# Values of one group directly behind the scores of the next: a change of the order of work around eight PSUM banks

## The chip, the cores and the metric

The kernel runs on one core of a Trainium2 chip. The metric is the device time of one execution in microseconds, median of several; all runs told here are of the same (fast) state, except `e8_before_again`, a single run whose state is not known. Engines are called as in the profile: PE is TensorE, DVE is VectorE, ACT is ScalarE, POOL is GpSimd.

## The reference

Attention with a sliding window of 128 and four sink tokens, then a gated feed-forward block on its output:

```python
# q, k, v: batch 4, 8 heads, 768 tokens, head size 64; n_sink 4, window 128
scores = q @ k.T / sqrt(64)
keep = (key < 4) | ((0 <= query - key) & (query - key < 128))
a = softmax(where(keep, scores, -1e9)) @ v
x = a.transpose(0, 2, 1, 3).reshape(3072, 512)          # w_gate, w_val: 512x1536
out = (silu(x @ w_gate) * (x @ w_val)) @ w_out           # w_out: 1536x512
```

## The kernel before

Tokens come in 12 groups of 256 (g; three to a batch, c is the place in the batch), a group in two tiles of 128 (j). `step_S` makes the scores of one half of the heads and takes four PSUM banks, `step_K` the scores against the sink tokens, `step_PV` the values of one tile and one half of the heads:

```python
    def step_PV(g, j, hh, act=False):
        b, c = divmod(g, GC)
        ...
        po = bank([P, 4, D + 1], FP32, "o")
        mms = []
        if c > 0:
            mms.append((po, es_t[g][:, j * P:(j + 1) * P],
                        vsbs[b][:, 4 * hh:4 * hh + 4]))
        for hq in range(4):
            h = 4 * hh + hq
            if t > 0:
        ...
        for i, (o, l, r) in enumerate(mms):
            nc.tensor.matmul(o, l, r, start=(i == 0), stop=(i == len(mms) - 1),
                             skip_group_check=True)

        def dve():
            rcp = smallp.tile([P, 4, 1], FP32, tag="rcp", name="rcp")
            nc.vector.reciprocal(rcp, po[:, :, D:D + 1])
            ...                              # or on ScalarE, at the start
            nc.vector.tensor_tensor(
                xns[g, j][:, 256 * hh:256 * (hh + 1)].rearrange(
                    "p (h d) -> p h d", h=4),
                po[:, :, 0:D], rcp.broadcast_to([P, 4, D]), op=ALU.mult)
        later.append(dve)                    # runs at the next flush
```

The feed-forward block works in eight token blocks. A unit of it is a `gate`: projection pg, tanh on ScalarE, then whatever attention steps the plan puts there, then projection pv; VectorE forms u (from tanh and pg) and ht (from u and pv), and then does the attention's masks and normalisations that were put off:

```python
        pg = project(wgs, "pg")
        th = tpool.tile([P, 512], FP32, tag="th", name="th")
        nc.scalar.activation(th, pg, AF.Tanh, scale=0.5)
        for a in attn:
            a()
        pv = project(wvs, "pv")
        ...
            nc.vector.scalar_tensor_tensor(u, th, 1.0, pg, op0=ALU.add, op1=ALU.mult)
            nc.vector.tensor_tensor(hts[tb][...], u, pv, op=ALU.mult)
        ...
            product()
            flush()
```

All PSUM tiles come from one pool of eight banks (`psum = pool("psum", 8, True)`), and which bank a tile gets is settled when the program is built. The plan of the later stages spreads scores (two steps, two units apart) and values (four half tiles in four units):

```python
    def pair(ga, gb, sh=0):
        s = sh
        return [((s, s + 2), Ss(ga)), ((s + 4, s + 5, s + 6, s + 7), PVs(ga)),
                ((s + 6, s + 8), Ss(gb)),
                ((11, 11, 12, 12) if s else (10, 11, 12, 13), PVs(gb))]

    weave(gates(3) + downs(3), slots(
        (2, [K(5)]), *pair(5, 6, 2), (2, C(6)), (7, C(7)), (13, C(8))))
    weave(gates(4) + downs(4), slots(
        (0, sinks(2)), *pair(7, 8), (3, [K(7)]), (3, C(9)), (7, C(10)), (10, C(11))))
    weave(gates(5) + downs(5), slots(
        (0, sinks(3)), *pair(9, 10), (6, [K(10)])))
    weave(gates(6) + gates(7) + downs(6) + downs(7), slots(
        ((0, 2), Ss(11)), ((4, 5, 6, 7), PVs(11))))
```

I call the stretch from the first gate projection of token block 3 to that of block 4 "stage 3", and so on; the part after stage 5 is the "last part".

The softmax here doesn't subtract the row's maximum and nothing guards it: scores larger than these inputs give would overflow.

## Time and profile before

| | value |
|---|---|
| time, median of 3 | 242.3 us (241.95 to 242.7) |
| profiled span | 240.4 us, mean granted clock 0.993 |
| TensorE busy | 97% of the span |
| TensorE idle in stages 3 to 5 (78.66 to 187.43 us) | none: its view of waits in that window is empty |
| VectorE busy | 66% |

How to read such a page: TensorE's row is the one that counts, as it is busy all the time from 25 us on. There a removed matmul or a cheaper form gains its length, and a wait costs its length. The lines themselves are in the prediction.

### The profile page before, as it was taken

Reading aid. Unit: us, or ns where it says so; the run is one execution under the profiler, and the core shown is the slowest. Engines: PE = TensorE matmul, PEld = TensorE weight load, DVE = VectorE, ACT = ScalarE, POOL = GpSimd, SP = SyncE. Lnnn points to the kernel's source line nnn. Section 1 sums busy time; section 2 is a strip of 40 time slices with the busy share of each in tenths; the row PEclk is TensorE's granted clock in tenths of the full one; section 3 lists DMA queues with packets and bytes.
Section 4 is the critical chain, followed back from the end, with each engine's and each line's share of the span. In section 5 each row is a group of like instructions: output and inputs, shape, how many; then the busy total and the mean of one; then the engine's idle time right before and its main releaser. Section 6 shows DMA issues by size and latency. Waiting matters only on the chain.

```text
span 240.4 us, 5190 instructions
## 1 busy us (share of the span) xinstructions
PE 232.7 (97%) x2071; PEld 135.3 (56%) x2071; DVE 158.8 (66%) x334; ACT 112.6 (47%) x227; POOL 70.7 (29%) x92
## 2 busy tenths in 40 slices
PE   7799999999999999999999999999999999999994
PEld 3477887768745445454445454445454445488443
DVE  4569778939973589880698971498971599877000
ACT  2778447358451483621656611556611662332111
POOL 8985387686256745650000000000000000000000
PEclk9979999999999999999999999999999999999999
DMA  7999999999999999999920654200304200200132
GB/s 136 147 180 197 206 187 206 171 154 145 194 119 200 195 160 155 155 148 191 236 48 0 125 97 133 87 0 1 46 0 131 90 0 3 44 0 3 59 117 87
DMA packets 98793, 27.37 MB, mean 114 GB/s; under 512 B 84817, under 2 KB 95825, under 8 KB 98769
## 3 DMA queue, kind: packets, MB, share of 16 engines
q0 software_dynamic: 68832, 13.90, 71.5%
q1 hardware_dynamic: 29504, 12.75, 26.9%
q10 hardware_dynamic: 432, 0.39, 0.5%
q8 instruction: 16, 0.26, 0.5%
q14 instruction: 9, 0.07, 0.1%
HBM read 28.34 MB, written 6.29 MB: 144 GB/s over the span
## 4 chain that ended last, share of the span: by engine, by line
PE 87%; DVE 5%; ACT 3%; DMA 2%; issue 1%; DVEq 0%; ACTq 0%; POOLq 0%
PE pv L448 25%; PE pd L501 25%; PE pg L448 23%; PE o L384 5%; PE s L331 4%; PE pt L267 3%; ACT e L338 2%; DVE e L343 2%; DMA kq<-in_k_dram 2%; DVE ht L463 1%; DVE xn L396 1%; PE px L420 1%; DMA out_dram<-ot 1%; DVE u L462 1%; ACT xn L392 1%
## 5 line engine op out<-in xcount | busy, mean ns | idle before, releaser
L448 PE MATMUL pv<-xT,wv 128*128 128x256 bf16 (+1 forms) x384 | 74.4, 326 | 0.2 <-DVE xn L396 0.2
L448 PE MATMUL pg<-xT,wg 128*128 128x256 bf16 (+1 forms) x384 | 74.2, 326 | 0.0
L455 ACT ACTIVATE th<-pg 128x512 f32<-128x512 f32 x72 | 43.9, 609 | 59.7 <-PE pg L448 59.3
L462 DVE SCALAR_TENSOR_TENSOR u<-th,pg 128x512 bf16<-128x512 f32 x72 | 49.2, 683 | 30.5 <-ACT th L455 29.7
L501 PE MATMUL pd<-wo,ht 128*128 128x512 bf16 x276 | 63.4, 379 | 0.0
L463 DVE TENSOR_TENSOR ht<-u,pv 128x512 bf16<-128x512 bf16 x72 | 49.5, 687 | 10.2 <-PE pv L448 3.3
L448 PEld LDWEIGHTS <-wg 128*128 128x128 bf16 x384 | 37.4, 98 | 25.4 <-issue 0.2
L338 ACT ACTIVATE e<-s 128x512 bf16<-128x512 f32 (+1 forms) x96 | 46.3, 583 | 1.2 <-PE s L331 1.1
L448 PEld LDWEIGHTS <-wv 128*128 128x128 bf16 x384 | 34.1, 98 | 20.6 <-issue 2.7
L501 PEld LDWEIGHTS <-ht 128*128 128x128 bf16 x276 | 25.8, 98 | 28.0 <-issue 0.2
L505 ACT ACTIVATE ot<-pd 128x512 f32<-128x512 f32 x23 | 13.7, 597 | 53.0 <-PE pd L501 52.9
L343 DVE TENSOR_TENSOR e<-e,mask 128x1024 bf16<-128x1024 bf16 (+1 forms) x48 | 28.9, 641 | 1.2 <-ACT e L338 1.0
L123 POOL DMA_DIRECT2D va<-in_v_dram x24 | 21.2, 885 | 12.6 <-DMA kq<-in_q_dram 5.7
L384 PEld LDWEIGHTS <-e 128*128 128x128 bf16 x352 | 16.6, 99 | 6.7 <-DVE vcf L598 0.7
L396 DVE TENSOR_TENSOR xn<-o,rcp 128x256 bf16<-128x256 f32 x44 | 18.7, 424 | 2.5 <-DMA xT<-xn 1.0
L384 PE MATMUL o<-va,e 128*128 128x65 bf16 x352 | 18.2, 195 | 0.9 <-DVE vcf L598 0.5
L107 POOL DMA_DIRECT2D kq<-in_k_dram x16 | 14.1, 883 | 8.6 <-DMA kqT<-kq 4.5
L107 POOL DMA_DIRECT2D kq<-in_q_dram x16 | 14.1, 883 | 6.1 <-DMA va<-in_v_dram 2.9
L389 DVE RECIPROCAL rcp<-o 128x4 f32<-128x4 f32 x48 | 8.4, 176 | 6.8 <-PE o L384 6.8
L486 DVE TENSOR_SCALAR ot<-pd 128x256 f32<-128x256 f32 x1 | 0.4, 425 | 14.4 <-DMA out_dram<-ot 14.4
L331 PE MATMUL s<-kqT 64*128 64x128 bf16 (+1 forms) x168 | 9.4, 238 | 0.0
L272 DVE CAST qT<-pt 128x512 bf16<-128x512 f32 x7 | 4.7, 689 | 6.9 <-PE pt L267 6.9
(61 smaller groups left out, 107.5 us busy)
## 6 DMA issues: line engine op xcount, KB each, us to landing
out_dram<-ot SPq DMA_DIRECT2D x23, 256.0 KB
va<-in_v_dram POOLq DMA_DIRECT2D x24, 128.0 KB, 10.3
kq<-in_k_dram POOLq DMA_DIRECT2D x18, 128.0 KB, 9.3
kq<-in_q_dram POOLq DMA_DIRECT2D x16, 128.0 KB, 9.4
wo<-in_moe_w_out_dram POOLq DMA_DIRECT2D x4, 384.0 KB, 12.7
wg<-in_moe_w_gate_dram POOLq DMA_DIRECT2D x4, 256.0 KB, 8.7
wv<-in_moe_w_val_dram POOLq DMA_DIRECT2D x4, 256.0 KB, 9.1
kq<-in_k_dram POOLq DMA_DIRECT2D x3, 256.0 KB, 9.6
```

The lines of the kernel that those rows point to most:

```text
L107: nc.gpsimd.dma_start(x[:, j, i].rearrange("p (h d) -> p h d", d=D), src[b, :, t0:t0 + P].rearrange("h m d -> m h d"))
L123: nc.gpsimd.dma_start(va[:, j, :, 0:D], v[b, :, t0:t0 + P].rearrange("h m d -> m h d"))
L331: nc.tensor.matmul(pss[2 * pp + h][:, col:col + n * P], keys(b, t, r, p), queries(g, r, p, j, n), start=True, stop=True)
L338: nc.scalar.activation(e_t[g][:, h0 + h, lo:512], pss[2 * pp + h][:, lo:512], AF.Exp, scale=scale)
L343: nc.vector.tensor_tensor(e, e, m[:, :, lo:512].broadcast_to([P, 2, 512 - lo]), op=ALU.mult)
L384: nc.tensor.matmul(o, l, r, start=(i == 0), stop=(i == len(mms) - 1), skip_group_check=True)
L396: nc.vector.tensor_tensor(xns[g, j][:, 256 * hh:256 * (hh + 1)].rearrange("p (h d) -> p h d", h=4), po[:, :, 0:D], rcp.broadcast_to([P, 4, ...
L448: nc.tensor.matmul(ps[:, i * n:(i + 1) * n], ws[fi][:, c, fo * P:(fo + 1) * P], x[:, 0:n // P, c], start=(c == 0), stop=(c == DMC - 1))
L455: nc.scalar.activation(th, pg, AF.Tanh, scale=0.5)
L462: nc.vector.scalar_tensor_tensor(u, th, 1.0, pg, op0=ALU.add, op1=ALU.mult)
L463: nc.vector.tensor_tensor(hts[tb][:, f:f + two].rearrange("p a n -> p (a n)"), u, pv, op=ALU.mult)
L501: nc.tensor.matmul(po, hts[tb][:, f, ts * P:(ts + 1) * P], wos[f // n][:, f % n], start=(f == 0), stop=(f == DFC - 1))
```

## The change

The intent has two parts. At the start, more filler matmuls stand in group 0's waits, so that the clock stays whole, and the sink scores of group 1 come ahead of its second scores. Later, the values of a whole tile stand directly behind the scores of the next group: the scores leave the array in its 64-row form, and the two halves of the sink values, each needing 64 rows, run there side by side, into one bank each. So the whole tile's two value banks are taken at once, in a unit that already holds four banks of scores and two of projections.

```diff
     def step_PV(g, j, hh, act=False):
...
+    def step_PV2(g, j):
+        b, c = divmod(g, GC)
+        pos = [value_bank(g, j, hh) for hh in range(2)]
+        if c > 0:
+            for hh in range(2):
+                r = slice(64 * hh, 64 * (hh + 1))
+                nc.tensor.matmul(
+                    pos[hh], es_t[g][r, j * P:(j + 1) * P],
+                    vsbs[b][r, 4 * hh:4 * hh + 4],
+                    start=True, stop=False, skip_group_check=True)
+        for hh in range(2):
+            values(g, j, hh, pos[hh])
...
     first_T(0)
+    warm(3)
     step_S(0, 0, A(first_T, 1))
-    warm(1)
+    warm(3)
...
+    warm(2)                                 # after the first values of group 0
...
+    warm(3)                                 # between its last two value blocks
...
-        (0, [flush, A(step_S, 1, 1), K(1), A(next_load, 1)]), (2, [first_PVs]),
+        (0, [flush, K(1), A(step_S, 1, 1), A(next_load, 1)]), (2, [first_PVs]),
...
     weave(gates(3) + downs(3), slots(
-        (2, [K(5)]), *pair(5, 6, 2), (2, C(6)), (7, C(7)), (13, C(8))))
+        (2, [K(5)]), ((2, 4), Ss(5)), (2, C(6)), (7, C(7)),
+        ((8, 10), Ss(6)), ((8, 10), PV2s(5)), ((11, 12), PV2s(6)), (13, C(8))))
     weave(gates(4) + downs(4), slots(
-        (0, sinks(2)), *pair(7, 8), (3, [K(7)]), (3, C(9)), (7, C(10)), (10, C(11))))
+        (0, sinks(2)), ((0, 2), Ss(7)), (3, [K(7)]), (3, C(9)),
+        ((6, 8), Ss(8)), ((6, 8), PV2s(7)), (7, C(10)), (10, C(11)),
+        ((10, 12), Ss(9)), ((10, 12), PV2s(8))))
     weave(gates(5) + downs(5), slots(
-        (0, sinks(3)), *pair(9, 10), (6, [K(10)])))
-    weave(gates(6) + gates(7) + downs(6) + downs(7), slots(
-        ((0, 2), Ss(11)), ((4, 5, 6, 7), PVs(11))))
+        (0, sinks(3)), ((1, 3), PV2s(9)), ((2, 4), Ss(10)), (5, [K(10)]),
+        ((7, 9), Ss(11)), ((7, 9), PV2s(10)), ((11, 12), PV2s(11))))
+    weave(gates(6) + gates(7) + downs(6) + downs(7), {})
```

A reader should note that part of the attention work moved between stages (the scores of group 9 into stage 4, all of group 11 out of the last part), so that single stages cannot be compared before against after; their sum can.

More of the change, by code (lines that the diff above doesn't have):

```diff
@@ L367, in step_PV, with value_bank, values @@
         b, c = divmod(g, GC)
-        t = 2 * c + j
+        po = value_bank(g, j, hh)
+        if c > 0:
+            nc.tensor.matmul(
+                po, es_t[g][:, j * P:(j + 1) * P], vsbs[b][:, 4 * hh:4 * hh + 4],
+                start=True, stop=False, skip_group_check=True)
+        values(g, j, hh, po, act)
+    def step_PV2(g, j):
+        b, c = divmod(g, GC)
+        pos = [value_bank(g, j, hh) for hh in range(2)]
+        if c > 0:
+            for hh in range(2):
+                r = slice(64 * hh, 64 * (hh + 1))
+                nc.tensor.matmul(
+                    pos[hh], es_t[g][r, j * P:(j + 1) * P],
+                    vsbs[b][r, 4 * hh:4 * hh + 4],
+                    start=True, stop=False, skip_group_check=True)
+        for hh in range(2):
+            values(g, j, hh, pos[hh])
+    def value_bank(g, j, hh):
         if hh == 0:
             xns[g, j] = xnp.tile([P, DM], BF16, tag="xn", name="xn")
-        po = bank([P, 4, D + 1], FP32, "o")
+        return bank([P, 4, D + 1], FP32, "o")
+    def values(g, j, hh, po, act=False):
+        b, c = divmod(g, GC)
+        t = 2 * c + j
         mms = []
-        if c > 0:
-            mms.append((po, es_t[g][:, j * P:(j + 1) * P],
-                        vsbs[b][:, 4 * hh:4 * hh + 4]))
         for hq in range(4):
@@ L383, in step_PV @@
         for i, (o, l, r) in enumerate(mms):
-            nc.tensor.matmul(o, l, r, start=(i == 0), stop=(i == len(mms) - 1),
-                             skip_group_check=True)
+            nc.tensor.matmul(o, l, r, start=(c == 0 and i == 0),
+                             stop=(i == len(mms) - 1), skip_group_check=True)
         def dve():
@@ L644, with PV2s @@
         ((22, 22, 23, 23), PVs(4)), (24, Xs(4))))
-    def pair(ga, gb, sh=0):
-        s = sh
-        return [((s, s + 2), Ss(ga)), ((s + 4, s + 5, s + 6, s + 7), PVs(ga)),
-                ((s + 6, s + 8), Ss(gb)),
-                ((11, 11, 12, 12) if s else (10, 11, 12, 13), PVs(gb))]
+    def PV2s(g):
+        return [A(step_PV2, g, j) for j in range(2)]
     weave(gates(3) + downs(3), slots(
-        (2, [K(5)]), *pair(5, 6, 2), (2, C(6)), (7, C(7)), (13, C(8))))
+        (2, [K(5)]), ((2, 4), Ss(5)), (2, C(6)), (7, C(7)),
+        ((8, 10), Ss(6)), ((8, 10), PV2s(5)), ((11, 12), PV2s(6)), (13, C(8))))
     weave(gates(4) + downs(4), slots(
-        (0, sinks(2)), *pair(7, 8), (3, [K(7)]), (3, C(9)), (7, C(10)), (10, C(11))))
+        (0, sinks(2)), ((0, 2), Ss(7)), (3, [K(7)]), (3, C(9)),
+        ((6, 8), Ss(8)), ((6, 8), PV2s(7)), (7, C(10)), (10, C(11)),
+        ((10, 12), Ss(9)), ((10, 12), PV2s(8))))
     weave(gates(5) + downs(5), slots(
-        (0, sinks(3)), *pair(9, 10), (6, [K(10)])))
-    weave(gates(6) + gates(7) + downs(6) + downs(7), slots(
-        ((0, 2), Ss(11)), ((4, 5, 6, 7), PVs(11))))
+        (0, sinks(3)), ((1, 3), PV2s(9)), ((2, 4), Ss(10)), (5, [K(10)]),
+        ((7, 9), Ss(11)), ((7, 9), PV2s(10)), ((11, 12), PV2s(11))))
+    weave(gates(6) + gates(7) + downs(6) + downs(7), {})
 _INS = ['q', 'k', 'v', 'n_sink', 'window', 'moe_w_gate', 'moe_w_val', 'moe_w_out']
```

## The prediction

> **What bounds the kernel now.** I read the page's busy table first, then the waits of TensorE, the granted clock by window, and the timeline of TensorE around one scores block and one values block.
>
> ```profile
> PE 232.7 (97%) x2071; PEld 135.3 (56%) x2071; DVE 158.8 (66%) x334; ACT 112.6 (47%) x227; POOL 70.7 (29%) x92
> PE 87%; DVE 5%; ACT 3%; DMA 2%; issue 1%; DVEq 0%; ACTq 0%; POOLq 0%
> ```
>
> TensorE is busy for 97% of the span and is 87% of the chain that ended last. The other engines enter the chain almost only in the first 25 us:
>
> ```profile
> 9.53 2.32 ACT e L338 x6
> 11.87 0.56 DVE e L343
> 12.49 0.73 PE o L384 x10
> 13.22 1.00 PE pt L267 x24
> 14.21 0.97 PE px L420 x8
> 15.18 0.95 PE pt L267 x32
> 16.14 0.57 ACT kT L272
> ...
> 22.86 1.75 ACT xn L392 x8
> ```
>
> The columns are start, length, what. The transposes at 15.18 take 0.95 us for 32 pairs of heads; the reader should ask why, and the table by window answers (the last columns are granted clock, DMA share, GB/s):
>
> ```profile
> 9.00:10.80 1.80, 1.30 (x13) 0.68 (x12) 1.60 (x3) 1.80 (x5) 1.80 (x3) 1.00 1.33 156
> 10.80:12.40 1.60, 0.75 (x14) 0.47 (x12) 1.27 (x6) 1.60 (x7) 1.60 (x3) 1.00 1.30 169
> 12.40:15.80 3.40, 3.31 (x78) 2.86 (x82) 2.10 (x9) 2.21 (x8) 2.90 (x4) 0.50 1.80 174
> 15.80:25.00 9.20, 8.66 (x131) 6.78 (x124) 7.89 (x22) 7.91 (x22) 5.87 (x9) 1.00 1.48 196
> 114.50:151.50 37.00, 37.00 (x274) 18.22 (x273) 25.15 (x50) 17.65 (x33) 0.00 (x0) 1.00 0.50 108
> ```
>
> From 12.4 to 15.8 us the clock is halved, right after the stretch 10.8 to 12.4 in which TensorE was busy for only 0.75 of 1.60 us. And from 114.5 to 151.5 TensorE has no idle time at all: there only fewer or cheaper matmuls can help, and any new wait costs its full length.
>
> The timeline of that steady part gives the unit costs (start, length, group):
>
> ```profile
> 132.14 1.03 PE L448 MATMUL pg<-xT,wg 128*128 128x512 bf16 x4
> 133.09 0.62 PE L331 MATMUL s<-kqT 64*128 64x128 bf16 x12
> 133.64 1.04 PE L448 MATMUL pv<-xT,wv 128*128 128x512 bf16 x4
> 134.52 1.03 PE L448 MATMUL pg<-xT,wg 128*128 128x512 bf16 x4
> 135.38 1.03 PE L448 MATMUL pv<-xT,wv 128*128 128x512 bf16 x4
> 136.24 1.03 PE L448 MATMUL pg<-xT,wg 128*128 128x512 bf16 x4
> 137.11 0.27 PE L384 MATMUL o<-vsb,es 128*128 128x260 bf16 x1
> 137.22 0.41 PE L384 MATMUL o<-va,e 128*128 128x65 bf16 x8
> 137.46 1.02 PE L448 MATMUL pv<-xT,wv 128*128 128x512 bf16 x4
> ```
>
> Start to start, a projection half takes 0.86 us (135.38 to 136.24). From pg to scores it is 0.95: entering the 64-row form costs 0.09. The scores block takes 0.55; its 1,024 columns per half at 0.216 us per 512 need 0.43, so about 0.1 is spent on leaving. A half of values has no such cost: 0.11 for the sink matmul (137.11 to 137.22) and 0.24 for eight values, 0.35 in all.
>
> **What the Trainium skill says.** "TensorEngine Tiling (Array Packing)", Key Properties: changing the tiling mode drains the array, and tiles work independently. The trace agrees with the first: 0.09 to 0.1 us each way; the scores show the second, with 64-row pairs running together. The same page, Gotcha 1: different row tiles must write to different PSUM banks. The change obeys it, as the two halves have a bank each. "TensorE: Matmul & The Clock Gate", Part 1: the clock is granted by activity in windows of about 3.4 us and is half or full only. The trace shows 0.50 for 3.4 us after a sparse stretch of 3.4 us (9.0 to 12.4); which share of activity is enough is not stated. "Perfetto Trace Analysis", Consistent bubbles: they can mean that there is no PSUM for the next tile. The kernel before shows none; the change may.
>
> **The change part by part.**
>
> (1) Sink values as one 64-row pair. It reaches groups 5, 7, 8, 10 and 11 (6 and 9 begin a batch and have no separate sink part), two token tiles each, so ten pairs. Before, a tile took 2 x 0.35 = 0.70. Directly behind scores the array is already in 64-row form, the pair costs 0.11 once, and the exit cost only moves: 0.11 + 2 x 0.24 = 0.59, a saving of 0.11. By the order of TensorE's instructions this holds for seven pairs (5 and 7 both, 8 one, 10 both): -0.77. The second tile of 8 (scores and values sit at different places of a down projection) and both of 11 stand alone and pay two changes of form: 0.11 + 0.48 + 0.2 = 0.79 for 0.70, three times +0.09 = +0.27.
>
> (2) The sink scores of groups 10 and 11 move from behind scores to a place of their own, one more change of form: +0.1. Sum of the steady part: -0.4 us.
>
> (3) Filler. Five matmuls of 128x512 fit in idle time that exists (0.81 before the first scores, 0.50 before the second, 0.5 before the last values of group 0) and cost nothing. The last three stand between two values blocks on the chain: 3 x 0.216 = 0.65, of which about 0.3 is visible. Filler raises the activity between 9.0 and 12.4 from about 1.4 us (matmuls counted by their streaming) to about 2.1 of 3.4. If the clock then stays whole, the first transposes of group 1 (1.0 to 0.5) end at 14.0 instead of 14.15 in spite of the 0.3, the projection transposes are held by the last normalisation until about 14.5, and the second transposes end at 15.0 instead of 16.0: 1.0 us less. If it does not, the three fillers take 3 x 0.43 = 1.3 and the same point comes 0.75 later.
>
> (4) What of that reaches the end? The weights are the next limit: the second chunk of the value projection is issued at 11.3 and lands 8.7 later, at 20.0, and its first user starts at 20.07. This cannot move. After it, values no longer wait 0.36 for the sink exponentials (they are now ahead of the second scores' on ScalarE), and the normalisations behind VectorE's chain (masks at 20.8, then ScalarE's 1.75 us at 22.86) come about 0.9 earlier. I get 24.0 in place of 24.73 for the value projection after it: -0.7. With the clock lost: +0.5.
>
> (5) New waits for PSUM. Eight banks. A gate unit with scores and a whole values tile now takes pg, four scores, two values, pv, which is all eight; two units later comes the next such. VectorE is in order: in such a unit u waits for tanh, h for pv (2.1 + 0.2 us after pg ended), then two masks (0.60 each), then twice reciprocal and normalise (0.55), 5.2 us after pg ended. By the semaphores of the built program, in stage 3 the second sink matmul of group 5's second tile waits for the u of the unit between, ready at about 5.5, while TensorE is there at 5.0: 0.5. In stage 4 the sink matmuls wait for the normalisation of the unit two before: about 0.1, then 0.4. In stage 5: 0.2 and 0.1. Sum 1.3 if every wait counts in full; each stall also lets VectorE catch up, and the durations are known to a tenth only, so I take 0.6.
>
> **Sum.** -0.4 (array) -0.7 (start) +0.6 (PSUM) = -0.5 with the clock kept, so 241.8; +0.7 with the clock lost, so 243.0. I give the first about 0.7.
>
> **The rivals.** First, the PSUM wait swallows all: VectorE has 1.39 us of work per plain gate unit of 1.73, and 3.7 in a unit with scores and values of 3.0. For it speaks this ratio; against it that the down projections give VectorE 10 us of rest per stage. At its full 1.3 the time is 242.5, and 243.5 if each of the five pairs stalls by 0.5. Second, the clock dips all the same, because the window runs freely and its phase decides: 243. Third, the start does not matter: the weights that land at 20.0 absorb it wholly, and only the array saving is left: 241.9 without stalls, 242.5 with them. Fourth, the best case: no stalls and the whole 1.0 us reaches the end: 240.9. Spread of the kernel before is 241.95 to 242.7, so all these lie within or near its scatter.
>
> **Range and chances.** Predicted 241.8 us; 240.3 to 243.4 holds the cases above except the extremes. Two per cent is 4.8 us; no part of the sum has that size. Faster by over 2%: 0.02; within 2%: 0.96; slower: 0.02.
>
> **What would show it.** Right on (1): rows of o from vsb in 64-row form, with 0.11 from the pair's first start to the form change, and seven blocks of scores plus values about 0.1 shorter than 0.55 + 0.70. Right on (3): granted clock 1.00 between 12.4 and 15.8. Right on (4): the second chunk's value projection still starting near 20.0 and the one after the first values 0.7 earlier. Right on (5): idle time of TensorE before o or s, released by VectorE's u or xn, in stages 3 to 5, where there was none. The prediction is wrong if the clock dips again, if these idle times exceed 1.5 us together, or if leaving the 64-row form towards values costs more than towards a projection.

## The result, and the profile after

The changed kernel takes 245.2 us (median of 4, 244.86 to 245.6), the kernel before 242.5 us in the same rounds (median of 4, 241.95 to 242.89). The ratio is 1.0114, with a 95% interval of 1.0085 to 1.0142. Ratios here are the mean time of one kernel's fast runs over that of the other's fast runs of the same rounds, so not quite the ratio of the medians. It is slower by 1.1%: inside the 2% band, but outside the predicted range of 240.3 to 243.4.

First the page of the kernel after, its busy row and the chain that ended last by engine:

```profile
PE 234.7 (96%) x2067; PEld 134.0 (55%) x2081; DVE 159.2 (65%) x334; ACT 113.0 (46%) x227; POOL 70.8 (29%) x92
PE 83%; DVE 6%; ACT 6%; DMA 2%; issue 1%; DVEq 0%; ACTq 0%; POOLq 0%
```

TensorE fell from 87% to 83% of the chain, and VectorE and ScalarE rose by 1 and 3 points: the chain now passes through other engines more often. This is a weak sign, as e1_start_only below, which has none of the new waits, shows 73%. (The busy sum of TensorE rises by 2.0 us although the attention's work on it shrank: the filler's busy time alone went from 4.6 us in 11 matmuls to 7.0 in the 19 of its now 21 that the trace kept, and the ends of matmuls are modelled. Busy time is a poor witness here; starts are a good one.)

Two windows of the table by stretch, columns as in the prediction (length, busy of PE, PEld, DVE, ACT and POOL, granted clock, DMA share, GB/s):

```profile
12.40:15.80 3.40, 2.87 (x88) 2.07 (x86) 2.54 (x9) 2.72 (x11) 3.29 (x5) 1.00 1.88 170
114.50:151.50 37.00, 36.15 (x277) 16.84 (x278) 26.97 (x54) 20.23 (x40) 0.00 (x0) 1.00 0.45 92
```

The clock stays whole between 12.4 and 15.8, as hoped. But in the steady window, where TensorE had 37.00 of 37.00, it now has 36.15. The view of TensorE's waits from 78 to 193 us, empty for the kernel before, has four rows (who waits, for whom, us in total, times, longest):

```profile
PE o L382 <- ACT e L338: 1.1, 3, 0.4
PE o L406 <- DVE e L343: 0.5, 2, 0.3
PE o L382 <- DVE u L484: 0.3, 1, 0.3
PE pv L470 <- DVE ht L485: 0.2, 1, 0.2
```

L382 is the shared sink pair, L406 the values. The idle time printed, 2.1 us, is again only what the modelled ends leave over; the cost is read from start to start. TensorE's timeline of stage 4 has a good unit and a bad one close together:

```profile
128.56 0.62 PE L331 MATMUL s<-kqT 64*128 64x128 bf16 x12
129.01 0.27 PE L382 MATMUL o<-vsb,es 64*128 64x260 bf16 x2
129.22 0.66 PE L406 MATMUL o<-va,e 128*128 128x65 bf16 x16
129.72 1.02 PE L470 MATMUL pv<-xT,wv 128*128 128x512 bf16 x4
...
133.27 0.62 PE L331 MATMUL s<-kqT 64*128 64x128 bf16 x12
133.83 0.28 PE L382 MATMUL o<-vsb,es 64*128 64x260 bf16 x1
134.51 0.27 PE L382 MATMUL o<-vsb,es 64*128 64x260 bf16 x1 [0.40 <-ACT e L338]
134.71 0.66 PE L406 MATMUL o<-va,e 128*128 128x65 bf16 x16
135.21 1.02 PE L470 MATMUL pv<-xT,wv 128*128 128x512 bf16 x4
```

The first unit is what the change wanted: scores, pair and a whole tile of values in 1.16 us (128.56 to 129.72), with 0.21 from the pair's start to the values. The second takes 1.94 us (133.27 to 135.21): the second sink waits, and 0.78 us is lost. Stage 3 shows the same for its second tile, and another wait as well:

```profile
100.27 0.27 PE L382 MATMUL o<-vsb,es 64*128 64x260 bf16 x1 [0.28 <-DVE u L484]
...
103.24 0.24 PE L406 MATMUL o<-va,e 128*128 128x65 bf16 x2 [0.27 <-DVE e L343]
103.71 0.23 PE L406 MATMUL o<-va,e 128*128 128x65 bf16 x2 [0.23 <-DVE e L343]
```

In the last two rows the values of group 6, placed one unit after their scores, wait for VectorE's masks. Read start to start, against the same block without a wait, the stalls cost: 0.55 (pair at 99.38 to 100.97), 0.85 and 0.22 (the masks), 0.78 and 0.79 (stage 4), 0.28 (a projection that waits for ht) and 0.78 (stage 5), 4.25 us together.

What VectorE does at the bad unit of stage 4 is in its own timeline:

```profile
131.39 1.28 DVE L343 TENSOR_TENSOR e<-e,mask 128x1024 bf16<-128x1024 bf16 x2
...
133.69 0.68 DVE L484 SCALAR_TENSOR_TENSOR u<-th,pg 128x512 bf16<-128x512 f32 x1
134.47 0.69 DVE L485 TENSOR_TENSOR ht<-u,pv 128x512 bf16<-128x512 bf16 x1
...
136.27 0.69 DVE L485 TENSOR_TENSOR ht<-u,pv 128x512 bf16<-128x512 bf16 x1 [0.52 <-PE pv L470]
```

The u that frees the bank of the unit between starts at 133.69 and ends at 134.37, although its tanh had ended at 132.24 already: VectorE, in order, had the masks and the normalisations of the last dense unit ahead of it, and was 1.45 us late. The row blamed ScalarE (e L338) because the built program gives the second sink the bank of the unit's own first scores tile, whose exponential began at 133.86 and took about 0.6. Either bank is free only at 134.4 or 134.5. So the named releaser alone does not tell the cause.

Nor was ScalarE late. Its exponentials of the good unit and of the bad one:

```profile
129.16 2.06 ACT L338 ACTIVATE e<-s 128x512 bf16<-128x512 f32 x4
133.86 2.06 ACT L338 ACTIVATE e<-s 128x512 bf16<-128x512 f32 x4
```

They start 0.60 and 0.59 us after the scores (128.56 and 133.27). A sink that is given the bank of its own unit's first scores has to wait for the first of them, however early VectorE is. The bank tables of the built programs, which the releasers in the traces bear out, show which sinks that concerns: the three with stalls of 0.78, 0.79 and 0.78 in stages 4 and 5, 2.35 us together. The good unit's second sink, and that of stage 3 which lost 0.55, have the bank of the unit between, which VectorE's u frees. So two things are to be told apart in what follows: how late VectorE is, and which bank the built program gives.

For the rest of the text, this table has the length of the steady part (first gate projection of stage 3 to the end) and its start, each from the profiled run:

```
run                    stage 1 starts   stage 3   stage 4   stage 5   last part   steady part
before                     51.03         35.84     36.97     35.96      53.01       161.78
after                      50.86         37.01     39.40     38.73      50.27       165.41
e1_start_only              49.99         35.85     36.97     35.95      52.99       161.76
e2_steady_only             50.50         37.00     39.40     38.71      50.28       165.39
e3_pairs_apart             50.77         36.75     38.46     38.37      50.26       163.84
e4_whole_sinks             50.34         37.01     39.20     38.53      50.28       165.02
e5_four_apart              50.73         36.59     36.83     35.95      53.01       162.38
e6_no_masks                50.19         35.62     37.83     37.69      50.26       161.40
e7_masks_pool              52.69         37.01     39.46     38.46      50.28       165.21
e9_four_apart_early        51.17         38.60     36.83     35.95      52.99       164.37
e10_six_later              51.06         36.16     39.40     38.73      50.28       164.57
e11_one_group              50.25         35.84     36.83     35.95      53.01       161.63
e12_sinks_only             50.25         36.23     36.96     35.96      52.99       162.14
```

Stage 1 in its first column starts with the first gate projection after the first down projections. The steady part grew by 3.63 us; the start gained 0.17 in this pair of profiles.

### The profile page after: what moved, and what is told of

Same layout as the page of the kernel before. It is cut to its first block, busy times and chain, and to the rows that moved or that the text cites. A ratio compares the mean times of both kernels' runs of the same rounds, so it can differ in the third digit from the quotient of the medians.

```text
span 243.9 us, 5196 instructions
## 1 busy us (share of the span) xinstructions
PE 234.7 (96%) x2067; PEld 134.0 (55%) x2081; DVE 159.2 (65%) x334; ACT 113.0 (46%) x227; POOL 70.8 (29%) x92
## 4 chain that ended last, share of the span: by engine, by line
PE 83%; DVE 6%; ACT 6%; DMA 2%; issue 1%; DVEq 0%; ACTq 0%; POOLq 0%
PE pd L523 24%; PE pv L470 24%; PE pg L470 22%; PE o L406 4%; ACT e L338 3%; PE s L331 3%; PE pt L267 3%; DVE e L343 2%; DMA kq<-in_k_dram 2%; DVE ht L485 1%; DVE xn L418 1%; ACT th L477 1%; PE o L382 1%; DMA out_dram<-ot 1%; DVE u L484 1%
## 5 line engine op out<-in xcount | busy, mean ns | idle before, releaser
L523 PE MATMUL pd<-wo,ht 128*128 128x512 bf16 x264 | 61.9, 379 | 0.6
L470 PEld LDWEIGHTS <-wv 128*128 128x128 bf16 x384 | 35.3, 98 | 23.0 <-issue 2.2
L338 ACT ACTIVATE e<-s 128x512 bf16<-128x512 f32 (+1 forms) x96 | 46.2, 581 | 2.5 <-PE s L331 2.5
L406 PEld LDWEIGHTS <-e 128*128 128x128 bf16 x352 | 14.1, 98 | 8.2 <-issue 3.4
L406 PE MATMUL o<-va,e 128*128 128x65 bf16 x352 | 16.6, 194 | 1.2 <-DVE vcf L622 0.5
L107 POOL DMA_DIRECT2D kq<-in_k_dram x16 | 14.2, 886 | 11.6 <-DMA va<-in_v_dram 4.4
```

The source lines that it names most:

```text
L107: nc.gpsimd.dma_start(x[:, j, i].rearrange("p (h d) -> p h d", d=D), src[b, :, t0:t0 + P].rearrange("h m d -> m h d"))
L338: nc.scalar.activation(e_t[g][:, h0 + h, lo:512], pss[2 * pp + h][:, lo:512], AF.Exp, scale=scale)
L406: nc.tensor.matmul(o, l, r, start=(c == 0 and i == 0), stop=(i == len(mms) - 1), skip_group_check=True)
L470: nc.tensor.matmul(ps[:, i * n:(i + 1) * n], ws[fi][:, c, fo * P:(fo + 1) * P], x[:, 0:n // P, c], start=(c == 0), stop=(c == DMC - 1))
L523: nc.tensor.matmul(po, hts[tb][:, f, ts * P:(ts + 1) * P], wos[f // n][:, f % n], start=(f == 0), stop=(f == DFC - 1))
```

## The experiments

Theory: VectorE is the holder. It is in order, and in the stretch of dense units it hands PSUM banks (and masked exponentials) back later than TensorE asks for them. Rivals: the change of the array's form costs more than thought; the start (filler, clock) is what loses; the shared pair itself stalls. A fourth, the bank that the built program gives to the second sink, got no run of its own.

### The two parts alone

e1_start_only is the kernel before with the start of the kernel after:

```diff
+    warm(3)                     # and 1 -> 3, +2, +3, as in the change
-        (0, [flush, A(step_S, 1, 1), K(1), A(next_load, 1)]), (2, [first_PVs]),
+        (0, [flush, K(1), A(step_S, 1, 1), A(next_load, 1)]), (2, [first_PVs]),
```

> The kernel before with the new start alone (filler matmuls in group 0's waits, sink scores of group 1 ahead of its second scores). Bank theory (the loss comes from units that want scores, values and projections in all eight PSUM banks, so the start is a gain that the loss hides): the clock stays whole from 12.4 to 15.8 us and the time falls by 0.7 us to about 241.7. Rival (the start is itself part of the loss, filler on the chain): 242.4 or more.

Measured: 241.94 us (6 runs, 241.11 to 242.68; before 242.44 with 11), ratio 0.9976, interval 0.9952 to 1.0001. e2_steady_only is the kernel after with these lines undone:

> The changed kernel with the old start. Bank theory: the loss of 2.7 us plus the 0.7 us that the start gave, about 245.8 us, with TensorE idle or stretched by about 4 us in stages 3 to 5. Rival (the start is part of the loss): below 245.

Measured: 245.3 us (6 runs, 244.73 to 247.52), ratio 1.0132, interval 1.0097 to 1.0168; its steady part of 165.39 us is the kernel after's 165.41. So the loss is wholly in the steady part, and the start is worth a few tenths of a microsecond, at the edge of what these rounds can see.

### The shared pair, apart from the scores and in another form

e3_pairs_apart keeps all shared pairs but puts them into units without scores:

```diff
-        ((8, 10), Ss(6)), ((8, 10), PV2s(5)), ((11, 12), PV2s(6)), (13, C(8))))
+        ((8, 10), Ss(6)), ((6, 7), PV2s(5)), ((12, 13), PV2s(6)), (13, C(8))))
-        ((6, 8), Ss(8)), ((6, 8), PV2s(7)), ...  ((10, 12), Ss(9)), ((10, 12), PV2s(8))
+        ((6, 8), Ss(8)), ((4, 5), PV2s(7)), ...  ((10, 12), Ss(9)), ((11, 13), PV2s(8))
-        ((7, 9), Ss(11)), ((7, 9), PV2s(10)), ((11, 12), PV2s(11))))
+        ((7, 9), Ss(11)), ((6, 8), PV2s(10)), ((11, 12), PV2s(11))))
```

> The changed kernel with every whole values tile moved to a gate or down unit of its own, without scores in it; shared sinks kept, now paying two changes of form each. Bank theory: the stalls go, what remains is 10 x 0.09 + 0.1 us of changes of form less 0.7 us at the start: about 242.7 us. Rival (the 64-row sink pair, its weight loads or the change of form to values cost more than I took): 244.5 us or more, as every pair now pays it twice.

Measured: 243.66 us (6 runs, 243.08 to 244.19), ratio 1.0048, interval 1.0027 to 1.0069. A lone pair and its tile take 0.72, plus 0.10 for entering the form:

```profile
91.24 0.28 PE L382 MATMUL o<-vsb,es 64*128 64x260 bf16 x2
91.46 0.66 PE L406 MATMUL o<-va,e 128*128 128x65 bf16 x16
91.96 1.02 PE L470 MATMUL pv<-xT,wv 128*128 128x512 bf16 x4
```

(These are TensorE's rows; the projection before began at 90.28, and its 0.86 ended at 91.14.) That is 0.82 against 0.70 for two halves before: alone, the shared form costs. No pair waits any more; what is left are 0.54 us at the start of stage 4, for which my later placement of group 6 is probably to blame (the view names only TensorE's own down projections), and 0.21 for ht. These, and 0.12 instead of 0.09 for each of ten lone pairs, about make up the time over the expected 242.7. So a shared pair does not stall by itself.

e4_whole_sinks is the kernel after with each half's sink over the whole array (slice `r` taken away):

> The changed kernel with the sink values as two matmuls over the whole array in the same places. Bank theory: the stalls stay; seven pairs cost 0.11 us more, the three that stand alone 0.09 less, and four of the seven disappear in a wait that is there anyway: 245.2 to 245.7 us. Rival (the shared pair itself is slow): 244 us or less.

Measured: 244.94 us (6 runs, 244.14 to 246.55), ratio 1.011, interval 1.008 to 1.014: a little under the expected range, but far from the rival. The same stalls are at the same places, and the built program has the same banks. A unit that does not stall takes 1.16 (94.26 to 95.42), where the same unit of the kernel after takes 1.04 (94.79 to 95.83): the shared form saves 0.12 there. In the total nothing of it is seen, because in stalled units TensorE only waits longer, and in the lone pairs it costs. The form is cleared of the loss.

### Is it VectorE?

e6_no_masks is wrong (relative error 0.69): from group 5 on, VectorE's masks are left out, and nothing else:

```diff
-            later.append(dve)
+            if g < 5:
+                later.append(dve)
```

> Wrong result on purpose: the changed kernel without VectorE's mask multiplications from group 5 on (1.2 us less for VectorE in every unit with scores); TensorE's order is the same. Bank theory with VectorE as the holder: the banks come free before TensorE asks (u of the unit between at 4.7 us after the first gate instead of 5.9, asked for at 5.2), the stalls vanish, about 241.3 us. Rival (the wait is for ScalarE's exponentials of the same scores, as the waits name it, and VectorE has no part): the waits stay, 244 us or more.

Measured: 241.08 us (4 runs, 240.92 to 241.31), ratio 0.9943, interval 0.9921 to 0.9965. The unit that lost 0.78 is now, in TensorE's timeline:

```profile
131.20 0.62 PE L331 MATMUL s<-kqT 64*128 64x128 bf16 x12
131.65 0.28 PE L383 MATMUL o<-vsb,es 64*128 64x260 bf16 x2
131.86 0.66 PE L407 MATMUL o<-va,e 128*128 128x65 bf16 x16
132.36 1.02 PE L471 MATMUL pv<-xT,wv 128*128 128x512 bf16 x4
```

1.16 us, like the good one, and the view of TensorE's waits from 78 to 193 us is empty. The steady part is 161.40: 4.01 us less than in the kernel after, and 0.38 less than before. So the masks on VectorE are needed for all of the loss, and the array saving of 0.4 is really there underneath (the second profile of the kernel before, `e8_before_again`, has a steady part of 161.78 again).

By what way they cause it is shown for a part only. In stage 3 the second sink has the same kind of bank in both programs, the one that the u of the unit between frees. There, and for the values that wait for the masks themselves, VectorE's lateness is the cause: 0.55 and 1.07 us. In stages 4 and 5, 2.35 us, the built program without masks also has other banks: its second sinks now wait for the u of the unit between, as in stage 3, and that u comes in time. Two things changed at once, and no run has the one without the other. The trace of the kernel after suggests that another bank alone would have helped little, as the u in question ended at 134.37, only about 0.1 us before the exponential; that is an argument and no experiment.

e7_masks_pool gives the masks of groups 7 to 10 to GpSimd, which has nothing to do there:

```diff
-                nc.vector.tensor_tensor(
+                (nc.gpsimd if 7 <= g <= 10 else nc.vector).tensor_tensor(
```

> The changed kernel with the mask multiplications of groups 7 to 10 on GpSimd, which is idle from 115 us on; result correct. Bank theory: the two stalls of 0.8 us in stage 4 go and those of stages 3 and 5 stay, 243.6 us. Rival (ScalarE is the holder): 245 us as the changed kernel. Should GpSimd slow VectorE's own instructions, their mean durations show it and the gain is smaller.

Measured: 245.84 us (4 runs, 245.08 to 247.34), ratio 1.0146, interval 1.0112 to 1.018: a miss. The first two pairs of stage 4 did stop waiting (131.70 to 132.86 and 136.41 to 137.57 are 1.16 each), but with the banks of the u here too. In stage 5, where the masks of group 11 are still VectorE's and the second sink still has its own unit's first bank, the 0.78 stays (177.09 to 179.03). This fits both readings. And GpSimd takes 2.12 us for a mask that takes VectorE 0.69 (spans on GpSimd are rough); a unit of stage 4 waits for one of its masks and takes 1.45 instead of 1.04. While it runs, two tiny copies on VectorE hang (VectorE's timeline):

```profile
120.59 3.77 DVE L311 COPY ks<-kqT 64x16 bf16<-64x16 bf16 x2
```

Two copies take 3.77 us, where one takes 0.163 us in the kernel after. The Trainium skill, "SBUF — State Buffer", Terms, says that VectorE and GpSimd share a port pair which is held for the whole instruction, while the loser "fully blocks"; the trace agrees, with 1.88 us against 0.163. A projection then waits for VectorE, in TensorE's timeline:

```profile
125.12 1.02 PE L470 MATMUL pg<-xT,wg 128*128 128x512 bf16 x4 [1.07 <-DVE u L484]
```

So one wait was traded for another, and stage 4 takes 39.46 us, as long as in the kernel after. This profiled run, the slowest of the four, also had its clock whole only from 10.72 us on, which fits the late start in the table and has no part in the steady one.

### Distance

If VectorE is too slow for pairs two units apart, four units should do. e5_four_apart takes the new start and keeps only group 5 behind 6 and group 7 behind 8, four units apart; the rest is as before:

```diff
-        ((8, 10), Ss(6)), ((8, 10), PV2s(5)), ((11, 12), PV2s(6)), (13, C(8))))
+        ((6, 10), Ss(6)), ((6, 10), PV2s(5)), ((11, 11, 12, 12), PVs(6)), (13, C(8))))
-        ((6, 8), Ss(8)), ((6, 8), PV2s(7)), (7, C(10)), (10, C(11)), ...
+        ((5, 9), Ss(8)), ((5, 9), PV2s(7)), (7, C(10)), (10, C(11)), ((10, 11, 12, 13), PVs(8))))
```

> New start, and only groups 5 and 7 keep their values with shared sinks behind the scores of 6 and 8, in gate units four apart instead of two; all else placed as before the change. Bank theory (VectorE needs more than two units to give the banks back): no idle TensorE in stages 3 and 4, four pairs save 4 x 0.11 us on top of the start's 0.5: 241.5 us, 0.4 below the run of the start alone. Rival (values directly behind scores cost in themselves, at any distance): 242 us or more, with the idle times still in those four units.

Measured: 243.66 us (6 runs, 242.4 to 244.85), ratio 1.0053, interval 1.002 to 1.0087: a miss in time. No pair waits (units of 1.05 to 1.16 us), and stage 4 takes 36.83 us against 36.97 before. But stage 4 begins with a new wait in TensorE's timeline:

```profile
114.95 1.02 PE L470 MATMUL pg<-xT,wg 128*128 128x512 bf16 x4 [0.70 <-DMA xT<-xn]
```

The transposes of the normalised values are DMA work, and block 4 reads them. I put this down to my placement, but it is not shown: group 6's values stand in the same units as in the kernel before, and e12_sinks_only, with the placement of the kernel before, has the same wait at the same place (its stage 3 is 36.23 for 35.84). The wait does not explain the median either: the profiled run took 242.45 us, and three of the others took 244.26 to 244.85; those were not traced. e9_four_apart_early put group 6 one gate earlier to mend that (its expectation says "later" by mistake; the edit is as shown):

```diff
-        (2, [K(5)]), ((2, 4), Ss(5)), ...  ((6, 10), Ss(6)), ((6, 10), PV2s(5)), ((11, 11, 12, 12), PVs(6))
+        (1, [K(5)]), ((1, 3), Ss(5)), ...  ((5, 9), Ss(6)), ((5, 9), PV2s(5)), ((10, 10, 11, 11), PVs(6))
```

> The start of the kernel after; in the steady stages only two shared sink pairs behind scores (groups 5 and 7), four units apart from the next pair, and the scores and sink of group 6 put one gate later, so that its transposes have the time that the last such run (e5_four_apart) did not leave them. Theory (eight PSUM banks, handed back late by VectorE): no TensorE idle time at the values of stages 3 and 4, units of 1.04 to 1.16 us as in the run without masks, the 0.7 us wait for the transposes at the start of stage 4 gone, and a total some 0.4 us under e1_start_only: about 241.5 us. Rival (each placement buys a new wait somewhere, TensorE's order has no slack left to give): some wait of 0.5 us or more shows elsewhere and the time is 242.4 us or more.

Measured: 245.23 us (6 runs, 244.33 to 245.85), ratio 1.0109, interval 1.0081 to 1.0137: the rival's number. The scores of group 6 now come before the DMA transposes of its own keys have landed, and wait 2.14 us for them at 92.12; stage 3 takes 38.60. In stages 4 and 5 nothing waits (36.83 and 35.95). The theory's part on banks held; this place one gate earlier was too early for group 6.

e10_six_later is the kernel after with one number changed:

```diff
-        ... ((11, 12), PV2s(6)), (13, C(8))))
+        ... ((12, 12), PV2s(6)), (13, C(8))))
```

> The kernel after with one placement changed: the values of group 6 stand at the last gate, not one unit after their scores. Theory (those values waited for VectorE's two masks, which need 1.2 us and had one unit): the 1.07 us of two stretched units goes, nothing else changes, about 244.2 us, 0.995 to 0.997 of the kernel after. Rival (VectorE's total backlog sets the time, not the distance): the same wait shows one unit later and the time stays at 245.2 us.

Measured: 244.73 us (6 runs, 244.34 to 245.01), ratio to before 1.0088, interval 1.0063 to 1.0113. The wait for masks is gone and stage 3 is 0.85 us shorter (36.16 for 37.01); the expected 1.07 was a little high. Compared with the 1.0114 of the kernel after, which was measured in other rounds, the two intervals overlap, so the gain in time is only likely; in the profile it is plain.

e11_one_group adds to e1_start_only only group 7 behind 8:

```diff
-        (0, sinks(2)), *pair(7, 8), (3, [K(7)]), ...
+        (0, sinks(2)), ((0, 2), Ss(7)), ((5, 9), Ss(8)), ((5, 9), PV2s(7)), ((10, 11, 12, 13), PVs(8)), (3, [K(7)]), ...
```

> e1_start_only plus the one part of the change that no run so far has shown to stall: group 7's two tiles, as shared sink pairs behind the scores of group 8, four units apart. Theory (the array saving of the shared pair is real where no bank is waited for): stage 4 lasts 36.83 us from its first gate projection to the next stage's, as in both runs that had this arrangement, against 36.97 in e1_start_only; no TensorE idle time in stages 3 to 5; total 0.1 us under e1_start_only, about 241.8 us, ratio 0.995 to 1.000. Rival (two stalls were avoided only because something ahead of them was late): stage 4 of 37.3 us or more, and 242.3 us or more.

Measured: 241.97 us (6 runs, 241.05 to 243.35), ratio 0.9996, interval 0.9967 to 1.0025. Stage 4 is 36.83 for the third time and nothing waits from 78 us on. A tenth of a microsecond cannot be told from nothing by these times.

### The clock and the start

e8_before_again is the kernel before once more, for its clock:

> The kernel before, once more, for its granted clock. If the halved clock from 12.4 to 15.8 us belongs to the kernel, it is there again. If it hangs on where the clock's window happens to lie (the changed steady part with the old start had a whole clock all through), it may be gone, and the start's gain differs from run to run.

Measured: 242.23 us in one run, with the clock halved from 12.74 to 16.16. e12_sinks_only is the kernel before with the sink scores of group 1 first and no new filler:

> The kernel before with only the sink scores of group 1 ahead of its second scores; no extra filler. Theory (both parts of the start count: the order saves the values' wait for the sink exponentials, 0.36 us, the filler only guards the clock): the clock dips once between 12 and 16 us or not at all, by the moment at which it first became full; values of group 1 start without a wait; stage 1 starts 0.3 us or so earlier than in the kernel before, about 50.7 with the dip and 50.2 without; 242.1 us, 0.997 to 1.001. Rival (the order alone is all of the gain of e1_start_only): stage 1 starts at 50.0 and 241.7 us even with the dip.

Measured: 242.48 us (6 runs, 241.58 to 243.77), ratio 1.0009, interval 0.9982 to 1.0036. The values of group 1 no longer wait for the sink exponentials, as expected, but the time is that of the kernel before. Its clock did not dip, without the new filler. Nor did it in e2_steady_only, which also has the old filler. In the traces the clock first becomes whole between 4.18 and 10.72 us, at another moment in each run. Of the four profiled runs with the old filler, the two in which that moment was 5.60 and 5.92 us had the dip, the two with 6.45 and 6.54 did not; none of the ten with the new filler had it in its profile, although three of them became whole at 5.83 to 5.92 us as well. That leans to the filler, but is too few to call it the cause, and three timed runs of e9_four_apart_early, which has the new filler, show a mean clock of 0.991 to 0.993 again (where in the run is not known, as they were not traced). In the stage table, the old start without a dip gives 50.50, with the sinks' order 50.25, and with both parts 49.99 to 51.17 (leaving out the late clock of e7_masks_pool). So what the filler adds over the order is not shown; only e1_start_only as a whole leans to a gain. The record also says how little a dip matters to the time of the kernel before: of its 34 timed runs in these rounds, the 8 with a mean clock of 0.991 to 0.993 average 242.52 us and the other 26 average 242.35. (In e9_four_apart_early the three such runs are 1.15 us slower than the other three; why is open.)

No version beat the kernel before beyond doubt. e1_start_only, at 0.9976, is the best correct one.

## Why the prediction was wrong

**The array (steps 1 and 2) was right.** The sum of -0.4 us is what e6_no_masks shows in the steady part: -0.38. The single terms agree: 0.12 less for a pair behind scores (predicted 0.11), 0.82 for a lone tile (predicted 0.79).

**The clock (step 3) came out as guessed, for a reason that is not secured.** The filler run had a whole clock, but so had two runs without it. The step also put 1.2 us between a kept clock and a lost one (-0.7 against +0.5), where the 34 runs above show about 0.2; and its "five matmuls" in idle time are seven by the edit (three, two and two).

**The start (step 4) was too high.** -0.7 was predicted for what reaches the end. The value projection after the first values was put at 24.0 instead of 24.73 us; it starts at 24.55, because it follows its gate projection by 2.07 us where it followed by 1.84 before. The start of the kernel after is 0.17 earlier in its profile, and e1_start_only gains 0.24% of 242.4, some 0.6 us, with an interval that just includes nothing. The user of the second weight chunk, which "cannot move" from 20.0, starts at 19.99 in the kernel after, but at 19.35 in e1_start_only and 19.54 in e12_sinks_only. This scatter of the start from run to run, over 1 us in the table, was not in the working.

**The PSUM waits (step 5) are the step that failed.** The prediction took +0.6; the runs show +4.0 (165.41 less 161.40), 4.25 by hand from the starts. That banks come back too late was named rightly. One wait of the list was right in place and size, stage 3's for the u of the unit between: 0.5 predicted, 0.55 measured. The rest went wrong in three ways. First, for stages 4 and 5 the working let the sinks wait for VectorE's normalisations, 0.1 to 0.4 us each. The second sinks there have the bank of their own unit's first scores, which the working did not count as a wait at all, and lost 0.78, 0.79 and 0.78 us until ScalarE's exponential had read it. Second, the 1.07 us of group 6's values, one unit behind their scores with two masks to wait for, were not looked for, as they are no PSUM wait; nor were the 0.28 for ht. Third, the sum of 1.3 was halved because "each stall also lets VectorE catch up".

The figures that speak against the halving stand in the prediction itself: VectorE needs 1.39 us in a plain unit and 3.7 in a dense one, which makes 5.1 for two; TensorE, without stalls, needs 4.7 (127.60 to 132.31 for such two units). In that stretch VectorE falls behind by 0.4 us per two units, by this estimate. That is half of the 0.78, so throughput alone is not the account. Nor is VectorE full there: from 132.31 to 137.80, 5.49 us, it is busy for 4.80, and its ht waits 0.52 for the pv of the unit whose sink had waited (the row at 136.27). Each engine waits for the other in turn. The argument against the rival, that the down projections give VectorE 10 us of rest per stage, does not help: that rest comes after the stretch, and only eight banks bridge the time. With four units to a pair, VectorE needs 3 x 1.39 + 3.7 = 7.9 of about 8.2 us, and the second sinks there have the banks of the unit between; no pair waits in e5_four_apart and e11_one_group. Not tried were the second sinks in another bank with all else kept, and an order of VectorE's work with the next u ahead of the normalisations.

**The rivals.** "The PSUM wait swallows all", at 243.5 if each pair stalls by 0.5, was the right one, still 1.7 us short (five pairs at 0.5 with its other terms add up to 243.7, not 243.5). "The start does not matter" is close to what the profile shows. The stated sign of failure, idle times of more than 1.5 us together, is what happened (2.1 us printed); but most of it, 1.1 us, is released by ScalarE's exponentials and not by VectorE's u or xn, as the prediction had it.

## What to carry to other kernels

Before packing work into fewer units of the bounding engine, add up what the engine that frees the buffers must do in that very stretch, and compare it with the stretch's length, not with the whole span: here 65% busy on average stood against an estimated 108% (5.1 of 4.7 us). Count the buffers held at once. When a unit takes all of them, look up which buffer the built program gives to each tile: one that the same unit has only just filled cost 0.78 us here each time. When a wait appears, the releaser that the row names can be one of several that are equally late. Take work off the suspected holder and see whether the wait goes; then check that the built program has kept its buffers, or the run has changed two things.

## What the Trainium skill lacked or had wrong

- "TensorEngine Tiling (Array Packing)", Key Properties, says that a change of mode drains the array, without a duration: here it is 0.09 to 0.10 us for each entry, and 0.12 us saved where two sink matmuls share the rows behind scores (1.04 against 1.16 us).
- The same page, Gotcha 1, names the pressure on banks but not what it can cost: 0.55 to 0.79 us here for each pair two units after another, about five to seven times what the sharing saves.
- "TensorE: Matmul & The Clock Gate", Part 1, gives as its rule no idle gap over about 3.4 us, and tells of a second way, frequent short idle times between groups of matmuls. The dip of 12.43 to 15.84 us looks like the second: TensorE was busy for 2.05 of the 3.40 us before, its longest printed idle time being 0.53. Which share of activity is enough is not stated, and these runs do not settle it. That the window runs freely agrees: the clock became whole at 4.18 to 10.72 us.
- "SBUF — State Buffer", Terms, agrees with what was seen of the shared port pair; but for a blocked VectorE the page has only a ratio of 6.8 (under Who interferes with whom), with no durations. Here two copies of 0.163 us each took 3.77 us together beside GpSimd's masks of 2.12 us, a factor of 11.6.
- "Perfetto Trace Analysis", Consistent bubbles, does not say that the releaser that a profile names can be one of two that are equally late, or that a rebuilt program can have other banks: three waits named ScalarE's exponentials, and taking away VectorE's masks removed all three and moved the banks.
